# The decay of the recurrent state as a task of its own in a hand-written scheduler, with new ranks and look-ahead

## The chip, the cores and the metric

The kernel runs on one core of a Trainium2 chip. The metric is the device time of one execution in microseconds (us); smaller is better. Where several runs are given, the median counts.

## The reference

Two stages. First a linear recurrence for 4 batches, 8 heads, 768 steps and head size 48: a complex decay per step and per row of the state, normalised so that its magnitude stays below 0.999, and an outer product of key and value added at each step; the output is the query applied to the real part of the state. Then a feed-forward layer on the 3072 tokens of width 384, with 2048 hidden channels and a leaky ReLU.

```python
mag = np.sqrt(a_re * a_re + a_im * a_im)
scale = np.minimum(mag, 0.999) / (mag + 1e-06)
a_re_n, a_im_n = (a_re * scale, a_im * scale)
for t in range(S):
    ar, ai = (a_re_n[:, :, t, :, None], a_im_n[:, :, t, :, None])
    new_re = ar * S_re - ai * S_im
    new_im = ar * S_im + ai * S_re
    kv = np.einsum('bhd,bhe->bhde', k[:, :, t], v[:, :, t])
    S_re, S_im = (new_re + kv, new_im)
    y[:, :, t] = np.einsum('bhd,bhde->bhe', q[:, :, t], S_re)
...
h = x @ w_in
g = np.maximum(0.01 * h, h)
return g @ w_out
```

The weights come as 64-bit floats, and the kernel itself turns them into two 32-bit parts each, a high and a low one.

## The kernel before

The sequence is cut into 6 chunks of 128 steps. A chunk is done for two batches at a time, so there are 12 units of work, numbered n = 0 to 11; n = 0 and 1 are chunk 0 of the two pairs of batches, n = 2 and 3 chunk 1, and so on. Unit n and unit n - 2 share a state. For each unit:

- `prep(n)` turns the decays into running products and scales queries and keys with them. It is a long chain, mostly on VectorE (DVE) with steps on ScalarE (ACT). Its first half writes to the tiles sq, u, a and xs; its second half begins with the first write to the tile qkt, of which there is one, so that it waits until the relays of unit n - 1 have read it.
- `relay_of(n, 0)` and `relay_of(n, 1)` move queries and keys by DMA from qkt to the tile t (t96), with the channels of a head on the partitions.
- `attend(n)`: scores on TensorE (PE, tile att), a mask on DVE (asb, more), keys turned by PE and copied by ACT (kn, more), the output of the unit by PE (att from asb, v and from t, rst), split into a high and a low part x by ACT and DVE, and the new state: PE makes the sum of key times value, DVE adds it to the state rst (`summed_up`), and ACT multiplies the state by the decay of the chunk (`decayed`). `decayed` issues 8 ACT instructions for one batch, one per head, in one go. In chunk 0 there is no old state, and `decayed` reads the sum straight from PSUM.

Beside these, 21 weight units are converted (`convert(i)`, tiles stage_...: ACT, DVE, ACT, PE, ACT), in memory that later holds other tiles; a task that needs such memory waits for the conversions in it (`freed`). The feed-forward layer (`forward`, 12 groups of 256 tokens, one per unit) is one task on PE: `first(g, s)` makes a 512-wide block of hidden values in PSUM (ph), `hide` (ACT, DVE, ACT, DVE, tiles tg and hid) applies the leaky ReLU and splits the result, `second(g, s)` multiplies by the second weight matrix (po). There are two PSUM buffers for ph. `hide(0, s)` for s = 0 to 2 waits for the conversions whose stage memory the tile hid takes over. After the last preparations a check of the weights (wck) runs on DMA and ACT.

The order of the instructions on each engine is written by a planner at build time. Every part above is a `Task` that hands out its instructions step by step (`yield`), and `drive` picks the next step by a clock of estimated costs: it takes the earliest possible start t0, and then, among the steps for the same engine that could start before t0 plus a tolerance, the one of lowest rank:

```python
t0, first = min(free, key=lambda x: (x[0], x[1].rank))
near = [(t.rank, at, k) for k, (at, t) in enumerate(free) if t.lane == first.lane and at <= t0 + look(t.rank)]
t = free[min(near)[2]][1]
```

So a low rank goes first; `look(rank)` is how long an engine may stand idle for it. After each step the rank grows by the task's pace. `DUE` gives rank and pace of the preparations, `UNIT` rank of the first conversion and the distance between two conversions. On a step of one task behind its own earlier step on the same engine the planner puts a start 0.14 to 0.15 us after that engine is free. A step marked "+" is ready as soon as the engine is. On the chip each engine then runs its instructions in this order.

Of the kernel before, what the change touches and what calls it, by code (L numbers as in the profile page):

```python
# [13 lines left out]
AF = mybir.ActivationFunctionType  # L14
# [3 lines left out]
B, H, S, D = 4, 8, 768, 48  # L18
# [3 lines left out]
P = 128  # L22
C = 128
# [15 lines left out]
SUBS = [(0, (0, 1))]  # L39
# [17 lines left out]
QKT, T96, X0, X1, V, A, KN, STG, ST, HID = (0, 1), (2, 3), 4, 5, 6, 7, 8, 9, 10, (11, 12, 13)  # L57
# [12 lines left out]

TOKENS = [(c, b) for c, bs in SUBS for b in bs]

R_RELAY, R_ATT, R_HID, R_FF, R_WCK, R_FLAG = -4, -3, -2, 1000, 10000, 10001
DUE = [(-2, 0.0), (28, 0.7), (250, 0)]
UNIT = (-1.1, 0.5)
PLACE = (8, 10, 11)
LATE = 1
LOOK = {R_RELAY: 0.2, R_ATT: 0.3, -1: 0.16}
SOON = 0.06


def look(rank):
    return SOON if 0 < rank < 200 else LOOK.get(rank, 0.0)

TB = 2

# [70 lines left out]
def pe_costs():  # L157
    small = [False]

    def cost(name, kw, aps):  # L160
        out, n = aps[0], aps[0].free_size()
        tiled = out.partition_size() == 32
        turn = 0.13 if tiled != small[0] else 0.0
        small[0] = tiled
        if name == "transpose":
            each = 0.083
        elif tiled:
            each = 0.029 if n <= D else 0.008 + n * 0.00037
        else:
            each = n * 4 / 2400 if kw["lhsT"].dtype == F32 else n / 2400 + 0.0075  # L170
        return turn + each, turn + each + 0.17

    return cost
# [282 lines left out]
def body(ctx, tc, keep, a_in, qk_in, v_in, w_in, out):  # L456
# [25 lines left out]
    pe, dve, act = Lane(tc, nc.tensor, pe_costs()), Lane(tc, nc.vector, dve_cost), Lane(tc, nc.scalar, act_cost)  # L482
# [26 lines left out]
    banks = Banks(att)  # L509
# [43 lines left out]
    live = []  # L553
    fetched_a, fetched_qk, fetched_v, prepared, moved_q, moved_k, attended, hidden, stored, checked = ({} for _ in range(10))
    converted = []
    carried, scaled, spread, inverted, asked, opened, loading = ([Mark() for _ in SUBS] for _ in range(7))
    placed = {(n, k): Mark() for n in range(2, nsub) for k in range(len(PLACE))}
    cleared = [Mark() for _ in range(NT // GT)]
    summed = [Mark() for _ in range(NT // GT)]

    def task(gen, rank, pace=0.0, end=0.0):
        live.append(Task(gen, rank, pace, end))
        return live[-1]

    def due(n):
        return DUE[n] if n < len(DUE) else (DUE[-1][0] + n, 0)

    def attends_of(n):
        return [attended[n]]

    def fetch_a(n):
        yield "S", *([prepared[n - 2], moved_k[n - 2]] if n > 1 else freed(A) if n else []), *([loading[n - 1]] if n else [])
# [38 lines left out]
    def freed(*places):  # L611
        return [x for x, r in zip(converted, ROUND) if r in places]
# [296 lines left out]
    def slot_of(s, h):  # L909
        if h < 6:  # L910
            return 6 * (h % 2) + 3 * s + h // 2
        return 12 + 2 * s + h - 6
# [16 lines left out]
    def attend(n):  # L929
        c, bs = SUBS[n]  # L930
        nb = len(bs)
        u0 = SUB_POS[n] // C
        g = u0 // NGU
        carry = c < NCH - 1
        at = [[placed[n, k]] if n > 1 else [] for k in range(3)]
        once, late = n > 0, n < LATE
        halves = [(bi, hh) for bi in range(nb) for hh in range(2)]
        ps, am, kn, px, pu = {}, {}, {}, {}, {}
# [71 lines left out]
        def update(bi):  # L1010
            v = raw_v[n]
            flat = pu[bi].rearrange("p a b -> p (a b)")
            for h in range(H):
                o = VW + h * D
                for q in range(3):
                    mm(
                        flat[32 * q : 32 * q + 32, h * D : (h + 1) * D],
                        lhsT=kn[bi][:, h].rearrange("p l d -> p (l d)")[:, 32 * q : 32 * q + 32],
                        rhs=v[:, bi, o : o + D],
                        start=True,  # L1020
                        stop=True,
                    )
# [8 lines left out]
        def rest(bi):  # L1031
            xh, xl, x0 = xgroup(u0 + bi)
            dve.scalar_tensor_tensor(
                out=xl[:, :, x0 : x0 + C], in0=px[bi][:, 0:TI], scalar=XSC, in1=xh[:, :, x0 : x0 + C].bitcast(F32),
                op0=ALU.mult, op1=ALU.subtract,
            )
            split[u0 + bi].set(attended[n].end + 0.6)
            banks.give(px.pop(bi), attended[n].end + 0.6)

        def state(bi):  # L1040
            r0 = rst[:, bs[bi], 0, 0]
            return bass.AP(r0.tensor, r0.offset, [list(r0.ap[0]), [PAIR, H // 2], [64, 2], [1, D]])

        def fresh(bi):
            return pu[bi].rearrange("p a b -> p (a b)")[0:96, 0:DM].rearrange("p (k j e) -> p k j e", j=2, e=D)

        def summed_up(bi):
            dve.tensor_tensor(out=state(bi), in0=fresh(bi), in1=state(bi), op=ALU.add)
            banks.give(pu.pop(bi), attended[n].end + 0.6)

        def decayed(bi):
            t96 = relay[n][1]
            r = state(bi)
            src = fresh(bi) if c == 0 else r
            for h0 in (0, 1, 6):
                hn = 2 if h0 == 6 else 3
                s0 = slot_of(1, h0)
                for x in range(hn):
                    h = h0 + (x if h0 == 6 else 2 * x)
                    act.activation(  # L1060
                        r[:, h // 2, h % 2], src[:, h // 2, h % 2], AF.Copy, scale=t96[:, s0 + x, bi, C : C + 1]
                    )
            if c == 0:
                banks.give(pu.pop(bi), attended[n].end + 2.5)

        yield "P", moved_q[n], moved_k[n], *at[0], *(attends_of(n - 1) if n else [masked]), banks.some(4 if once else 1)
        scored = []
        for k, (bi, hh) in enumerate(halves):
            if k:
# [9 lines left out]
        if carry and not late:  # L1079
# [9 lines left out]
            yield "+N"  # L1089
            shown_to = after(act, 0.15)  # L1090
        yield "+P", shown_to, fetched_v[n], banks.some(2 if late or not carry else 4), *at[2], *(
            [summed[g - 2]] if g > 1 else freed((X0, X1)[g])
        )
        for bi in range(nb):
            px[bi] = banks.take()
# [17 lines left out]
        for bi in range(nb):  # L1113
            yield "+V", rounds[bi]
            rest(bi)
        if not carry:
            return
        if late:
            for bi in range(nb):
# [8 lines left out]
            for bi in range(nb):  # L1128
                yield "+P" if bi else "P", banks
                pu[bi] = banks.take()  # L1130
                update(bi)
        for bi in range(nb if c else 0):
            yield "+V"
            summed_up(bi)
        for bi in range(nb):
            yield "+A" if bi else "A"
            decayed(bi)

    NS = NFC // NF
    shown = {}  # L1140
# [111 lines left out]
    masked = task(masks(), R_HID, end=4.5)  # L1252
    for n in range(nsub):
        fetched_a[n] = task(fetch_a(n), UNIT[0] + 5.5 * UNIT[1] if n == 1 else R_RELAY + 0.5)
        fetched_qk[n] = task(fetch_qk(n), R_HID if n else UNIT[0] + 2.5 * UNIT[1])
        prepared[n] = task(prep(n), *due(n))
        if n == 0:
            for i in range(NU):
                converted.append(task(convert(i), UNIT[0] + i * UNIT[1]))
        fetched_v[n] = task(fetch_v(n), R_RELAY - 1 if n else UNIT[0] + 9.5 * UNIT[1])  # L1260
        moved_q[n] = task(relay_of(n, 0), R_RELAY)
        moved_k[n] = task(relay_of(n, 1), R_RELAY)
        attended[n] = task(attend(n), R_ATT)
# [90 lines left out]
```

## Time and profile before

| what | us |
|---|---|
| median of 3 runs | 603.14 |
| lowest, highest run | 597.68, 604.97 |
| the profiled execution, its own time | 599.82 |
| span of the profiled execution | 598.1 |
| PE busy, DVE busy, ACT busy in it | 551.6, 522.6, 388.4 |

The span is the time from the first to the last instruction of the profiled execution. A busy PE is one with a matmul in its pipeline; the columns of a view are said where its rows stand.

### The profile page before, as it was taken

The numbers are of one execution on the slowest core, as the hardware profiler recorded it, in microseconds if no ns is written. First come the engines' busy times: TensorE is split into PE (matmuls) and PEld (weight loads), VectorE is DVE, ScalarE is ACT, GpSimd is POOL, SyncE is SP. The second block draws the span as 40 slices with busy tenths as digits, with TensorE's granted clock in tenths as the row PEclk, the third lists the DMA queues.
The fourth block names the chain that finished last, engine by engine and source line by source line (L and its number), as shares of the span: only waits on it lengthen the run. The fifth ranks groups of instructions, "written<-read, shape, count | busy, mean of one in ns | idle before, by whom it ended". The sixth has DMA issues, their size and how long they took to land.

```text
span 598.1 us, 17875 instructions
## 1 busy us (share of the span) xinstructions
PE 551.6 (92%) x7650; PEld 522.3 (87%) x7650; DVE 522.6 (87%) x897; ACT 388.4 (65%) x862; POOL 5.0 (1%) x23
## 2 busy tenths in 40 slices
PE   3865699999979899999999999999999999998996
PEld 2433499989969899999999999999999998998996
DVE  5999989999989999889999999999999998764232
ACT  7988586475474584584583674764755756775975
POOL 2000000000000000000000000000000000000000
PEclk9895799999999999999999999999999999999999
DMA  8973612522522423234235125125134266356650
GB/s 347 391 234 95 203 59 55 161 85 55 169 76 63 153 83 109 108 106 133 99 101 159 61 80 161 61 82 160 59 95 147 66 175 182 124 157 214 216 180 29
DMA packets 28370, 79.18 MB, mean 132 GB/s; under 512 B 3200, under 2 KB 9344, under 8 KB 28288
## 3 DMA queue, kind: packets, MB, share of 16 engines
q1 hardware_dynamic: 28288, 78.02, 41.1%
q8 instruction: 60, 0.98, 0.7%
q14 instruction: 22, 0.18, 0.1%
HBM read 54.26 MB, written 4.72 MB: 99 GB/s over the span
## 4 chain that ended last, share of the span: by engine, by line
PE 58%; DVE 20%; ACT 11%; DMA 7%; issue 3%; SPq 0%; DVEq 0%; ACTq 0%
PE po L121 21%; PE ph L121 20%; PE att L121 15%; DVE qkt L121 5%; DVE a L121 4%; DMA wck<-in_w_dram 3%; ACT wck L121 3%; DVE tg L121 2%; DMA t<-qkt 2%; DVE u L121 2%; DVE hid L121 2%; ACT rst L121 2%; DVE sq L121 1%; PE pd L121 1%; ACT tg L121 1%
## 5 line engine op out<-in xcount | busy, mean ns | idle before, releaser
L121 PE MATMUL ph<-x,win_hi 128*128 128x256 f32 x1152 | 215.7, 279 | 5.3 <-DVE tg L121 2.0
L121 PE MATMUL po<-hid,wout_hi 128*128 128x256 f32 x1152 | 215.3, 280 | 0.0
L121 PEld LDWEIGHTS ph<-x,win_hi 128*128 128x128 f32 x1152 | 181.4, 188 | 6.9 <-DVE tg L121 2.4
L121 PEld LDWEIGHTS po<-hid,wout_hi 128*128 128x128 f32 x1152 | 180.7, 188 | 1.6 <-issue 0.4
L121 PE MATMUL ph<-x,win_lo 128*128 128x256 f32 x576 | 141.6, 278 | 0.0
L121 PE MATMUL po<-hid,wout_lo 128*128 128x256 f32 x576 | 137.3, 278 | 0.0
L121 PEld LDWEIGHTS po<-hid,wout_lo 128*128 128x128 f32 x576 | 108.5, 188 | 0.0
L121 PEld LDWEIGHTS ph<-x,win_lo 128*128 128x128 f32 x576 | 108.4, 188 | 0.0
L121 ACT CAST hid<-tg 128x512 fp32r<-128x512 f32 x96 | 59.2, 616 | 52.7 <-DVE tg L121 50.9
L121 DVE TENSOR_TENSOR tg<-ph,tg 128x512 f32<-128x512 f32 x96 | 66.0, 687 | 30.5 <-ACT tg L121 30.4
L121 ACT ACTIVATE tg<-ph 128x512 f32<-128x512 f32 x96 | 56.7, 591 | 39.2 <-PE ph L121 38.9
L121 DVE TENSOR_TENSOR hid<-tg,hid 128x512 fp32r<-128x512 f32 x96 | 66.1, 688 | 14.2 <-ACT hid L121 13.3
L121 DVE TENSOR_TENSOR u<-a 128x384 f32<-128x384 f32 x84 | 46.6, 555 | 1.7 <-ACT a L121 0.2
L121 DVE TENSOR_TENSOR qkt<-qk,a 128x768 f32<-128x768 f32 x48 | 44.4, 956 | 2.6 <-ACT qkt L121 2.6
L121 PE MATMUL att<-t 96*32 96x96 f32 (+3 forms) x1536 | 36.9, 254 | 4.1 <-DMA t<-qkt 3.9
L121 PEld LDWEIGHTS att<-t 96*32 96x32 f32 x1536 | 33.8, 145 | 7.7 <-DMA t<-qkt 4.6
L121 PE MATMUL att<-t,rst 96*32 96x128 f32 x640 | 34.4, 272 | 1.6 <-issue 1.6
L121 ACT ACTIVATE wck<-wck 128x1152 f32<-128x1152 f32 (+1 forms) x22 | 27.2, 1238 | 11.5 <-DMA wck<-in_w_dram 11.4
L121 PE MATMUL att<-asb,v 128*32 128x128 f32 x592 | 33.9, 274 | 0.3 <-issue 0.3
L121 ACT ACTIVATE rst<-rst,t 96x48 f32<-96x48 f32 x128 | 29.8, 321 | 4.6 <-DVE rst L121 4.4
L121 DVE TENSOR_TENSOR a<-u 128x192 f32<-128x192 f32 x84 | 29.9, 356 | 1.9
L121 ACT ACTIVATE sq<-a 128x1536 f32<-128x1536 f32 x12 | 17.9, 1495 | 15.4 <-DMA a<-in_a_dram 15.4
(161 smaller groups left out, 769.8 us busy)
## 6 DMA issues: line engine op xcount, KB each, us to landing
t<-qkt SPq DMA_DIRECT2D x48, 290.2 KB, 4.2
wck<-in_w_dram SPq DMA_DIRECT2D x10, 1152.0 KB, 5.7
v<-in_v_dram SPq DMA_DIRECT2D x12, 832.0 KB, 4.7
a<-in_a_dram SPq DMA_DIRECT2D x12, 768.0 KB, 4.6
qk<-in_qk_dram SPq DMA_DIRECT2D x12, 768.0 KB, 5.9
out_dram<-ot SPq DMA_DIRECT2D x12, 384.0 KB, 2.7
t<-qkt SPq DMA_DIRECT2D x24, 129.0 KB, 4.1
stage_st<-in_w_dram SPq DMA_DIRECT2D x3, 768.0 KB, 4.5
```

The lines of the kernel that those rows point to most:

```text
L121: x = getattr(self.engine, name)(*args, **kw)
```

## The change

The decay leaves `attend` and becomes a task `fade` that issues one ACT instruction per step, 16 in a unit, with rank `R_FADE` = -3.142. `attend(n)` ends before it. The mark `faded[n]` stands for its end: the load of v and the relay of the queries of the next unit wait for it as they waited before for the end of `attend`, and the output matmuls of unit n wait for `faded[n - 2]` where they depended through the order of the units before; the scores of the next unit no longer wait for the decay. In chunk 0 (n = 0 and 1) the sum is first copied from PSUM to the state by ACT, one copy per batch, and the decay then reads the state in SBUF: 4 copies are added in all, and 32 of the 160 decays read another memory.

The ranks are set anew. `prep(0)` keeps -2 but now sinks by 0.078 a step, `prep(1)` goes from 28 (pace 0.7) to -9.02 (pace 0.201), the later ones from 250, 253, 254 ... to 244.623, 280.36, 284.36 ...; the conversions go from -1.1 + 0.5 i to 1.423 + 0.702 i. The tolerances change too: 0.2 to 0.417 for relays, 0.3 to 0.087 for attention, 0 to 0.199 for the steps of `hide` and `store`, 0 to 0.122 for all other negative ranks, 0.06 to 0.105 for ranks between 0 and 200.

```diff
-R_RELAY, R_ATT, R_HID, R_FF, R_WCK, R_FLAG = -4, -3, -2, 1000, 10000, 10001
-DUE = [(-2, 0.0), (28, 0.7), (250, 0)]
-UNIT = (-1.1, 0.5)
+R_RELAY, R_ATT, R_HID, R_FADE, R_FF, R_WCK, R_FLAG = -4, -3, -2, -3.142, 1000, 10000, 10001
+DUE = [(-2, -0.078), (-9.02, 0.201), (244.623, 0), (280.36, 0)]
+UNIT = (1.423, 0.702)
...
-LOOK = {R_RELAY: 0.2, R_ATT: 0.3, -1: 0.16}
-SOON = 0.06
+LOOK = {R_RELAY: 0.417, R_ATT: 0.087, R_HID: 0.199}
+EARLY, SOON, LATER = 0.122, 0.105, 0
 def look(rank):
-    return SOON if 0 < rank < 200 else LOOK.get(rank, 0.0)
+    if rank in LOOK:
+        return LOOK[rank]
+    return EARLY if rank < 0 else SOON if 0 < rank < 200 else LATER if rank < 900 else 0.0
...
     def attends_of(n):
-        return [attended[n]]
+        return [attended[n], faded[n]]
...
-        def decayed(bi):
+        def fade():
             t96 = relay[n][1]
...
+            for bi in range(nb):
+                r = state(bi)
+                for h in range(H):
+                    yield "+A" if bi or h else "A"
                     act.activation(
-                        r[:, h // 2, h % 2], src[:, h // 2, h % 2], AF.Copy, scale=t96[:, s0 + x, bi, C : C + 1]
+                        r[:, h // 2, h % 2], r[:, h // 2, h % 2], AF.Copy, scale=t96[:, slot_of(1, h), bi, C : C + 1]
                     )
-            if c == 0:
-                banks.give(pu.pop(bi), attended[n].end + 2.5)
+            yield "+N"
+            faded[n].set(act.clock + 0.3)
...
-        yield "P", moved_q[n], moved_k[n], *at[0], *(attends_of(n - 1) if n else [masked]), banks.some(4 if once else 1)
+        yield "P", moved_q[n], moved_k[n], *at[0], *([attended[n - 1]] if n else [masked]), banks.some(4 if once else 1)
...
-        for bi in range(nb if c else 0):
-            yield "+V"
-            summed_up(bi)
         for bi in range(nb):
-            yield "+A" if bi else "A"
-            decayed(bi)
+            yield "+V" if c else "A"
+            if c:
+                summed_up(bi)
+            else:
+                act.copy(state(bi), fresh(bi))
+                banks.give(pu.pop(bi), attended[n].end + 0.6)
+        yield "+N"
+        task(fade(), R_FADE, end=attended[n].end)
```

## Rows read from the trace of the kernel before

**Rows 1.** The page: busy time by engine; the span in 40 slices, busy tenths.
```profile
PE 551.6 (92%) x7650; PEld 522.3 (87%) x7650; DVE 522.6 (87%) x897; ACT 388.4 (65%) x862; POOL 5.0 (1%) x23
...
PE   3865699999979899999999999999999999998996
...
DVE  5999989999989999889999999999999998764232
...
```

**Rows 2.** Windows of the whole core: stretch, length, busy time of each engine.
```profile
0.00:77.40 77.40, 48.20 (x328) 27.95 (x329) 70.01 (x117) 61.18 (x115) 3.80 (x13) 0.85 0.70 246
77.40:165.00 87.60, 84.86 (x1222) 82.84 (x1223) 84.06 (x150) 52.21 (x129) 0.24 (x2) 1.00 0.34 102
165.00:250.00 85.00, 78.37 (x1231) 76.17 (x1225) 79.76 (x134) 50.28 (x123) 0.24 (x2) 1.00 0.34 102
250.00:500.00 250.00, 249.04 (x3834) 246.27 (x3822) 238.97 (x404) 156.30 (x375) 0.72 (x6) 1.00 0.37 110
```

**Rows 3.** Window of DVE alone before the feed-forward starts: stretch, length, busy time.
```profile
7.00:77.40 70.40, 68.08 (x110) 0.83 0.69 243
```

**Rows 4.** Timeline of DVE, 33 to 69 us: start, length, operation, [idle before it].
```profile
33.26 0.56 DVE L121 SCALAR_TENSOR_TENSOR stage_hid<-stage_hid 128x384 int32<-128x384 int32 x1
...
53.62 2.43 DVE L121 SCALAR_TENSOR_TENSOR stage_hid<-stage_hid 128x384 int32<-128x384 int32 x5
...
68.60 0.56 DVE L121 SCALAR_TENSOR_TENSOR stage_stg<-stage_stg 128x384 int32<-128x384 int32 x1
```

**Rows 5.** Timeline of SP and PE: relay of keys, first scores, first feed-forward matmul.
```profile
62.37 4.00 SPq L121 DMA_DIRECT2D t<-qkt  x5
...
68.50 3.67 PE L121 MATMUL att<-t 96*32 96x128 f32 x128
...
77.44 0.28 PE L121 MATMUL ph<-x,win_hi 128*128 128x256 f32 x1
```

**Rows 6.** Timeline of DVE, 77 to 106 us: operations of prep(1).
```profile
77.55 0.56 DVE L121 TENSOR_TENSOR u<-a 128x384 f32<-128x384 f32 x1
...
83.80 0.33 DVE L121 TENSOR_TENSOR xs<-u 128x48 f32<-128x48 f32 x2
...
86.17 1.75 DVE L121 TENSOR_TENSOR qkt<-a 128x1536 f32<-128x1536 f32 x1
...
103.98 1.83 DVE L121 TENSOR_TENSOR qkt<-qk,a 128x768 f32<-128x768 f32 x2
```

**Rows 7.** Timeline of ACT: two blocks of decays, and what follows the second.
```profile
122.40 3.10 ACT L121 ACTIVATE rst<-att,t 96x48 f32<-96x48 f32 x16
...
171.95 3.73 ACT L121 ACTIVATE rst<-rst,t 96x48 f32<-96x48 f32 x16 [2.42 <-DVE rst L121]
175.58 0.57 ACT L121 ACTIVATE tg<-ph 128x512 f32<-128x512 f32 x1
```

**Rows 8.** Timeline of DVE: the wait just behind the first of these blocks.
```profile
125.99 1.76 DVE L121 TENSOR_TENSOR qkt<-a 128x1536 f32<-128x1536 f32 x1 [0.55 <-ACT a L121]
```

**Rows 9.** The chain that ended last: its stretches of decays; start, length, what.
```profile
122.50 3.01 ACT rst L121 x16
...
173.32 2.35 ACT rst L121 x10
...
216.70 1.58 ACT rst L121 x7
...
467.45 3.48 ACT rst L121 x15
```

**Rows 10.** Groups of ACT: a copy of 384 columns; count, busy, mean ns.
```profile
L121 ACT COPY kn<-att 128x384 f32<-128x384 f32 x20 | 8.8, 481 | 7.4 <-PE att L121 7.3
```

**Rows 11.** Timeline of PE, 115 to 182 us: three of the gaps.
```profile
117.58 0.31 PE L121 MATMUL att<-ident,t 96*128 96x96 f32 x1 [0.88 <-issue]
...
124.45 0.74 PE L121 MATMUL ph<-x,win_hi 128*128 128x256 f32 x4 [0.93 <-DVE x L121]
...
176.93 0.39 PE L121 MATMUL ph<-x,win_hi 128*128 128x256 f32 x1 [1.74 <-DVE tg L121]
```

More of the change, by code (lines that the diff above doesn't have):

```diff
@@ L555, in body @@
     converted = []
-    carried, scaled, spread, inverted, asked, opened, loading = ([Mark() for _ in SUBS] for _ in range(7))
+    faded, carried, scaled, spread, inverted, asked, opened, loading = ([Mark() for _ in SUBS] for _ in range(8))
     placed = {(n, k): Mark() for n in range(2, nsub) for k in range(len(PLACE))}
@@ L1049, in summed_up @@
             banks.give(pu.pop(bi), attended[n].end + 0.6)
-        def decayed(bi):
+        def fade():
             t96 = relay[n][1]
[L1053 to L1059, printed above, removed]
+            for bi in range(nb):
+                r = state(bi)
+                for h in range(H):
+                    yield "+A" if bi or h else "A"
                     act.activation(
-                        r[:, h // 2, h % 2], src[:, h // 2, h % 2], AF.Copy, scale=t96[:, s0 + x, bi, C : C + 1]
+                        r[:, h // 2, h % 2], r[:, h // 2, h % 2], AF.Copy, scale=t96[:, slot_of(1, h), bi, C : C + 1]
                     )
-            if c == 0:
-                banks.give(pu.pop(bi), attended[n].end + 2.5)
-        yield "P", moved_q[n], moved_k[n], *at[0], *(attends_of(n - 1) if n else [masked]), banks.some(4 if once else 1)
+            yield "+N"
+            faded[n].set(act.clock + 0.3)
+        yield "P", moved_q[n], moved_k[n], *at[0], *([attended[n - 1]] if n else [masked]), banks.some(4 if once else 1)
         scored = []
@@ L1091, in attend @@
         yield "+P", shown_to, fetched_v[n], banks.some(2 if late or not carry else 4), *at[2], *(
-            [summed[g - 2]] if g > 1 else freed((X0, X1)[g])
+            [summed[g - 2], faded[n - 2]] if g > 1 else freed((X0, X1)[g])
         )
@@ L1116, in attend @@
         if not carry:
+            faded[n].set(attended[n].end)
             return
```

## The prediction

> **What bounds the kernel now.** I read the page first, then the windows, then the timelines around the start of the feed-forward layer, and the chain last. On the page PE is busy 551.6 and DVE 522.6 of 598.1 us, and the digits of the slices change places: DVE stands at 9 from the second slice on to about 500 us, PE only from the sixth or seventh, and at the end PE stays at 9 while DVE falls [rows 1]. The windows give this in numbers [rows 2]. Until 77.4 us the feed-forward layer has not begun and PE is idle for 77.4 - 48.2 = 29.2 us. From 77.4 to 250 us PE is idle for 2.7 + 6.6 = 9.4 us, from 250 to 500 us for 1.0 us. So from 250 us on PE is the bound, and whatever it has not done by then comes at the end. Before 250 us it is DVE that holds PE back: from 7 to 77.4 us it is idle for 70.4 - 68.1 = 2.3 us [rows 3], and from there to 250 us for 3.5 + 5.2 = 8.8 us [rows 2]. The change takes no DVE instruction away. What a new order can win is therefore bounded: DVE can finish the work that PE waits for at most 2.3 + 8.8 = 11.1 us sooner, if all its idle time in this stretch went and PE could use it. ACT is busy 65% [rows 1] and counts only where its queue delays one of the other two.
>
> **The decay as a task.** The same 160 multiplications remain. Rank -3.142 lies below attention (-3), `hide` (-2) and all later preparations (244 and more), and a low rank goes first. A step of `fade` is marked "+", so it is ready the moment ACT is free, when nothing else on ACT can start earlier. Every time one of the 16 steps is to be chosen, it wins; only `prep(1)` in its first 30 steps and the later part of `prep(0)` rank lower, and these are over by then. So I expect the 16 decays of a unit to stand together in ACT's queue as before: a block of 3.10 us in chunk 0 and 3.73 us behind [rows 7], begun at the same event, the state's sum from DVE. What waits behind it is the same: the activation that empties ph comes at 175.58 us right after a block, and PE gets its next buffer at 176.93 us after a wait of 1.74 us [rows 7, 11]. Value taken: 0. The bound on the gain is the block's whole place in the chain, 3.01 + 2.35 + 1.58 + 3.48 = 10.4 us [rows 9]; the bound on the loss is nothing, for no decay is added. The scores of the next unit lose a wait that was over long before in the order of the queue: 0.
>
> **Chunk 0.** Four copies of 96 x 384 from PSUM are added. A copy of 384 columns takes 481 ns [rows 10], two of them about 0.85 us as they overlap. The 16 decays behind now read SBUF, as those of the later chunks: 3.73 instead of 3.10 us [rows 7]. Together 0.85 + 0.63 = 1.5 us of ACT for each of units 0 and 1. After the block of unit 1 DVE waits 0.55 us for an ACT copy that stood behind it [rows 8], so 1.5 us more lands on DVE there. For unit 0 the same can happen to the first `hide`. Bounds 0 and 3.0 us; I take 1.0, since PE has gaps of its own in this stretch [rows 11] that swallow a part.
>
> **prep(1) before the conversions.** This is the real reordering. Before, `prep(1)` with rank 28 filled what prep(0), attention and the conversions left. After 33.26 us DVE still has 24 conversion operations, 14.6 us, the last at 68.60 us [rows 4]; they alternate with prep(0), whose next step is never ready at once, and one run of five takes 2.43 us where prep(0) waits for ACT [rows 4]. The feed-forward layer starts at 77.44 us, after the scores of unit 0 (68.50 us) [rows 5]. So the conversions have 77.4 - 69.2 = 8.3 us in hand. Now `prep(1)` takes these places. How much is it? At 77.55 us its first half has only the operations up to 83.80 us to go, about 5.6 us without the one `tg` and the gap in them; its second half, 12 operations from 86.17 to the two that start at 103.98 us, sums to 13.3 us [rows 6]. The second half cannot start before the relay of unit 0 has read qkt, 62.37 + 4.00 us and a landing later [rows 5]. So at most 5.6 + 13.3 = 18.9 us of DVE work can come in front of conversions that PE and `hide` need, and 8.3 us of this are in hand. The other 10.6 us are the bound on a later start of group 0. But that work is only moved: after group 0 DVE has as much less to do for unit 1, whose attention then fits inside group 0, and PE's 9.4 us of gaps until 250 us shrink by what it lost before. The net lies between +10.6 - 9.4 = +1.2 us and the gain of the gaps of unit 1, 0.88 + 0.93 us [rows 11] and a little more, if the start does not move. I take -2.0 us: each step of `prep(1)` needs 0.14 us after its last, so conversions still get every other place, and I expect the start within 4 us of 77.4.
>
> **The tolerances.** On a chain within one engine a next step is ready after 0.14 us, and 0.122 and 0.105 us are below that, so there they change nothing. They act where a step comes from another engine: DVE may idle up to 0.199 us for a `hide` step rather than begin a preparation of about 1 us. PE does 163.2 of the 503.4 us that it works after 77.4 us before 250 us [rows 1, 2], a third, so some 32 of the 96 hidden blocks lie there; two DVE steps for each, 0.2 us each, are 12.8 us if all waited. An estimate: a step arrives inside a window of 0.2 us before an operation of 1 us one time in five, and half the window is waited, so 64 x 0.2 x 0.1 = 1.3 us. Against that, PE's blocks come sooner by the operation not put before them, and attention waits less (0.087 for 0.3 us). Bounds +3 and -5 us; I take -1.0. The new ranks from prep(2) on keep their order among themselves: 0.
>
> **The sum.** 599.82 + 0 + 1.0 - 2.0 - 1.0 = 597.8 us against the profiled execution. The median of the runs is 3.3 us higher and the lowest run 2.1 us lower; a median of the new kernel may fall anywhere in that spread. I forecast 598 us. No change that a measurement can tell reaches from 591 to 615 us, 2% to either side of the median of 603.14.
>
> **Rivals.** (1) The hand-out does what it says: the activations of `hide` slip between the decays, the four places in the chain go [rows 9], and DVE's waits behind them too. The page "Perfetto Trace Analysis" of the Trainium skill, section Optimizing Scalar/DVE Operations, says that where Scalar and Vector are not saturated but cause bubbles on other engines, breaking up instructions may let work finish sooner; the decays are separate instructions already, so by that rule the gain is that of the order. With all DVE idle time as its ceiling the time is 599.8 - 10.4 = 589.4 us, with the tolerances 585 to 591. For it: the 1.74 us gap of PE behind a block [rows 7, 11]. Against: the rank. Chance 0.2. (2) The slow one: the conversions of the stage memory used two and three times, which `hide(0, s)` and the keys of unit 0 wait for, slip behind all 18.9 us of `prep(1)`. Group 0 stops for want of hid, unit 0's attention ends late, and the relay for unit 1 waits for it. It decides from the point where PE's gaps until 250 us, 9.4 us [rows 2], no longer take the delay up. With the 10.6 us of above wholly lost the time is 599.8 + 10.6 = 610 us; if prep(0) too is held, because `prep(1)` ranks below it for its first 20 steps, the 8.3 us in hand do not count and all 18.9 us are lost, 619 us. For it: DVE has no idle time there [rows 3]. Against: the alternation. Chance 0.12. (3) Nothing measurable moves, since DVE is as full as before and everything is only exchanged: 600 to 604 us; this is so near the forecast that they share one chance, 0.68.
>
> **How the numbers follow.** The forecast with rival 3 reaches from 592 to 607 us. To leave no more than 2 in 10 out, the range goes into rival 1 down to 587 and into rival 2 up to 611. Below 591 us lie most of rival 1 and a little of the forecast: 0.18. Above 615 us lies the upper end of rival 2: 0.05. The rest, 0.77, is within 2%.
>
> **What would show it.** Decays in the new trace: 16 in one block, about 3.7 us also in chunk 0, with 4 copies of 384 columns to rst before the first two; if `tg` or `hid` stand between them, rival 1 is right. First matmul of ph between 75 and 82 us; beyond 88 us, rival 2. The second half of prep(1) done by about 90 us instead of 105.8. DVE idle before 250 us still 8 to 13 us, and PE idle from 250 to 500 us about 1 us. I am wrong if PE's gaps after 250 us grow, for then the later ranks, which I put at nothing, have moved something, or if the total of PE's busy time itself changes.

## The result, and the profile after

The changed kernel takes 609.14 us (median of 4 runs, 606.59 to 610.73) against 601.78 us of the kernel before beside it (4 runs, 597.68 to 604.97): ratio 1.0123, 95% interval 1.0081 to 1.0165. It is slower by a little over 1%, inside the forecast range and within the 2%, where I had forecast 598 us, a gain. The profiled execution after took 609.05 us, its span is 607.3 us; before 599.82 and 598.1 us.

The page of the changed kernel (busy time by engine; busy tenths in 40 slices; the group of the decays), beside [rows 1]:

```profile
PE 552.4 (91%) x7650; PEld 522.2 (86%) x7650; DVE 521.4 (86%) x897; ACT 390.6 (64%) x866; POOL 5.0 (1%) x23
...
PE   4763599989999989999999999999999999998995
...
DVE  5999899979969999999999999999898998864232
...
L123 ACT ACTIVATE rst<-rst,t 96x48 f32<-96x48 f32 x160 | 37.2, 321 | 1.1 <-DVE rst L123 1.1
```

PE's busy time has grown by 0.8 us, the span by 9.2; nearly all of it is idle time of PE. Where, the windows say (stretch, length, busy time of PE, PEld, DVE, ACT, POOL; then the granted clock of TensorE as a share of full speed, the share of the DMA engines, GB/s), beside [rows 2]:

```profile
0.00:77.40 77.40, 43.40 (x250) 23.89 (x250) 68.07 (x117) 57.83 (x107) 3.80 (x13) 0.80 0.67 240
77.40:165.00 87.60, 83.37 (x1163) 80.53 (x1162) 79.77 (x134) 54.75 (x133) 0.24 (x2) 0.98 0.33 103
165.00:250.00 85.00, 81.28 (x1263) 78.86 (x1262) 77.80 (x133) 49.77 (x125) 0.24 (x2) 1.00 0.34 101
250.00:500.00 250.00, 247.56 (x3766) 244.89 (x3766) 239.39 (x406) 154.65 (x376) 0.60 (x5) 1.00 0.33 100
```

From 77.4 to 250 us DVE, the engine that holds PE back there, is idle for 7.8 + 7.2 = 15.0 us; before it was 8.8 us. Two waits of DVE make 7.8 us of it. Its timeline shows them (start, length, operation, [idle before it, and what ended it]), with the operation ahead of each wait:

```profile
127.17 1.76 DVE L123 TENSOR_TENSOR qkt<-a 128x1536 f32<-128x1536 f32 x1 [0.54 <-ACT a L123]
132.17 1.76 DVE L123 TENSOR_TENSOR a<-a 128x1536 f32<-128x1536 f32 x1 [3.24 <-ACT a L123]
...
173.32 0.32 DVE L123 TENSOR_TENSOR xs<-u 128x48 f32<-128x48 f32 x2
178.19 1.76 DVE L123 TENSOR_TENSOR qkt<-a 128x1536 f32<-128x1536 f32 x1 [4.56 <-issue]
```

The first stands in prep(2), beside the attention of unit 1, the second in prep(3), beside unit 2. What DVE waits for is read on ACT's timeline at the same times (the last two lines are from the end of the kernel):

```profile
124.79 0.85 ACT L123 COPY rst<-att 96x384 f32<-96x384 f32 x2
126.72 0.36 ACT L123 COPY a<-xs 128x96 f32<-128x96 f32 x1 [1.09 <-DVE xs L123]
126.90 3.71 ACT L123 ACTIVATE rst<-rst,t 96x48 f32<-96x48 f32 x16
130.52 0.90 ACT L123 ACTIVATE ot<-po 128x256 f32<-128x256 f32 x3
131.31 0.58 ACT L123 ACTIVATE tg<-ph 128x512 f32<-128x512 f32 x1
131.79 0.35 ACT L123 COPY a<-xs 128x96 f32<-128x96 f32 x1
...
172.96 3.72 ACT L123 ACTIVATE rst<-rst,t 96x48 f32<-96x48 f32 x16 [1.08 <-DVE rst L123]
176.59 0.90 ACT L123 ACTIVATE ot<-po 128x256 f32<-128x256 f32 x3
177.39 0.54 ACT L123 COPY a<-xs 128x96 f32<-128x96 f32 x2
...
600.26 0.94 ACT L123 ACTIVATE ot<-po 128x256 f32<-128x256 f32 x3 [1.50 <-PE po L123]
601.07 1.31 ACT L123 ACTIVATE wck<-wck,low 128x1152 f32<-128x1152 f32 x1
```

`prep` ends its first half with two copies a<-xs of 96 columns; DVE goes on only behind them. In unit 1 the block of 16 decays has come between the two, with ot and tg behind it; in unit 2 the block and ot stand ahead of both. The second wait is put down to "issue", but the copies end at 177.39 + 0.54 = 177.93 us, 0.26 us before DVE goes on. That it waits for them is inferred from ACT's timeline; in the kernel before the view names them for the same operation, with a wait of 0.54 us (last line below). The kernel before had the same block [rows 7], but in unit 2 not in that place; its ACT timeline, and one line of DVE's:

```profile
165.45 0.54 ACT L121 COPY a<-xs 128x96 f32<-128x96 f32 x2 [1.61 <-DVE xs L121]
...
591.29 1.36 ACT L121 ACTIVATE wck<-wck,low 128x1152 f32<-128x1152 f32 x1
...
592.97 0.94 ACT L121 ACTIVATE ot<-po 128x256 f32<-128x256 f32 x3 [0.24 <-PE po L121]
...
165.90 1.76 DVE L121 TENSOR_TENSOR qkt<-a 128x1536 f32<-128x1536 f32 x1 [0.54 <-ACT a L121]
```

There the copies of prep(3) begin 6.5 us before the block does, at 171.95 us [rows 7]. With the new ranks the last xs comes at 173.6 us and not at 165.4, while the block begins only 1 us later than before: the preparation has moved behind the attention, and the block is ready first.

The starts of the scores of each unit on PE (us) show what these places cost; the last columns are two experiments of below:

| unit | before | after | fourth | thirteenth |
|---|---|---|---|---|
| 0 | 68.5 | 74.0 | 74.5 | 74.3 |
| 1 | 111.0 | 112.7 | 114.0 | 113.1 |
| 2 | 154.7 | 158.6 | 156.7 | 152.2 |
| 3 | 196.4 | 204.0 | 196.5 | 194.6 |
| 5 | 281.4 | 289.1 | 282.4 | 281.6 |

After is 1.7 us late at unit 1, 3.9 at unit 2, 7.6 at unit 3 and 7.7 at unit 5. The rest arises at the end: from the start of the last ot to the end of the span it is 598.1 - 592.97 = 5.1 us before and 607.3 - 600.26 = 7.0 us after. 7.7 + 1.9 is about the 9.2 us. PE shows both: its gap behind the first wait of DVE, where [rows 11] had 1.74 us at the most, and its last wait, before the flag of the check:

```profile
134.59 0.39 PE L123 MATMUL ph<-x,win_hi 128*128 128x256 f32 x1 [2.65 <-DVE tg L123]
...
603.82 0.19 PE L123 MATMUL att<-scr 128*1 128x1 f32 x2 [3.48 <-DVE scr L123]
```

In the kernel before that last wait is 1.02 us. The windows show one thing more that the prediction had no term for, the granted clock of TensorE; the first line is the kernel before, the others the changed one:

```profile
77.40:593.00 515.60, 503.19 (x7322) 494.24 (x7320) 451.42 (x768) 326.13 (x744) 1.20 (x10) 1.00 0.38 116
```
```profile
135.20:138.60 3.40, 3.40 (x19) 3.40 (x18) 3.40 (x6) 3.18 (x5) 0.00 (x0) 0.50 0.00 0
138.60:142.00 3.40, 3.40 (x31) 3.40 (x31) 2.84 (x5) 2.80 (x5) 0.00 (x0) 1.00 0.07 19
...
558.50:561.90 3.40, 3.40 (x50) 2.95 (x43) 1.54 (x3) 2.98 (x8) 0.00 (x0) 0.50 0.14 16
```

Before the change the clock is full, 2.4 GHz, from 77.4 us to the last po. In the changed kernel it is at half, 1.2 GHz, in two stretches: one begins just behind the gap of 2.65 us, the other just behind a gap of 2.00 us that ends at 557.26 us. In the first PE comes to 19 matmuls of ph and po, in the next 3.40 us at full clock to 31; by this the first stretch costs some 1.3 us, an estimate.

### The profile page after: what moved, and what is told of

Read it like the earlier page. It is cut to its first block, busy times and chain, and to the rows that moved or that the text cites. A ratio compares the mean times of both kernels' runs of the same rounds, so it can differ in the third digit from the quotient of the medians.

```text
span 607.3 us, 17861 instructions
## 1 busy us (share of the span) xinstructions
PE 552.4 (91%) x7650; PEld 522.2 (86%) x7650; DVE 521.4 (86%) x897; ACT 390.6 (64%) x866; POOL 5.0 (1%) x23
## 4 chain that ended last, share of the span: by engine, by line
PE 44%; DVE 9%; ACT 5%; DMA 2%; issue 2%; SPq 1%; DVEq 0%; ACTq 0%
PE po L123 18%; PE ph L123 17%; PE att L123 9%; DVE qkt L123 2%; DMA wck<-in_w_dram 2%; ACT wck L123 2%; DVE tg L123 1%; ACT rst L123 1%; DVE a L123 1%; SPq L123 1%; DVE hid L123 1%; DVE u L123 1%; ACT hid L123 1%; DVE sq L123 1%; DVE xs L123 1%
## 5 line engine op out<-in xcount | busy, mean ns | idle before, releaser
L123 ACT ACTIVATE rst<-rst,t 96x48 f32<-96x48 f32 x160 | 37.2, 321 | 1.1 <-DVE rst L123 1.1
L123 PE MATMUL att<-t 96*32 96x32 f32 (+3 forms) x1536 | 34.9, 250 | 1.0 <-DMA t<-qkt 0.9
L123 PEld LDWEIGHTS att<-t 96*32 96x32 f32 x1536 | 32.4, 144 | 3.7 <-DMA t<-qkt 1.6
L123 ACT ACTIVATE x<-att 128x384 fp32r<-128x384 f32 x24 | 11.8, 492 | 26.8 <-PE att L123 26.8
```

What stands on the lines that cost most here:

```text
L123: x = getattr(self.engine, name)(*args, **kw)
```

## The experiments

Three theories were set against each other. A: the block of decays stands on ACT ahead of small operations that DVE waits for. B: `prep(1)` pushes the conversions back, the feed-forward layer starts later (81.28 us, before 77.44 [rows 5]), and that start is lost. C: the task itself, its copies and marks, costs. "Before" is the kernel before on the same chip.

**1. The ranks alone.** The kernel before with the new ranks and tolerances; the decay stays in `attend`.

```diff
-DUE = [(-2, 0.0), (28, 0.7), (250, 0)]
-UNIT = (-1.1, 0.5)
+DUE = [(-2, -0.078), (-9.02, 0.201), (244.623, 0), (280.36, 0)]
+UNIT = (1.423, 0.702)
...
-LOOK = {R_RELAY: 0.2, R_ATT: 0.3, -1: 0.16}
+LOOK = {R_RELAY: 0.417, R_ATT: 0.087, R_HID: 0.199}
```

> The kernel before with the new ranks and tolerances alone; the decay stays in attend. Theory A (the loss is the block of decays standing on ACT in front of two small copies a<-xs that DVE waits for, at units 1 and 2): here the block stands before one pair of copies only (unit 1), one DVE wait of about 3 us instead of two of 3.2 and 4.6 us, so 604 to 606 us. Theory B (prep(1) pushes the conversions back and the feed-forward starts later, 81.3 instead of 77.4 us): all of the loss, 608 to 610 us. Theory C (the task itself, its rank above attention and its four copies): none of it, 601 to 603 us.

Measured 625.22 us (622.42 to 629.55), ratio 1.0346, 1.0263 to 1.0429: worse than any of the theories said. From unit 3 to unit 9, seven times, ACT and DVE show the same picture:

```profile
348.45 3.72 ACT L123 ACTIVATE rst<-rst,t 96x48 f32<-96x48 f32 x16 [2.81 <-DVE rst L123]
352.07 0.58 ACT L123 ACTIVATE tg<-ph 128x512 f32<-128x512 f32 x1
352.55 0.53 ACT L123 COPY a<-xs 128x96 f32<-128x96 f32 x2
```
```profile
352.68 0.69 DVE L123 TENSOR_TENSOR tg<-ph,tg 128x512 f32<-128x512 f32 x1 [3.17 <-ACT tg L123]
```

Here tg and both copies stand behind the block in each unit, and DVE waits 3.2 to 3.6 us each time; in the kernel before it has no wait over 1.1 us from 77 to 300 us. It is theory A in a larger dose, and it needs no task. From the first ph to the last po PE is also busy for 512.2 us with the matmuls that take it 504.9 us in the changed kernel, at a mean granted clock of 0.98 for 0.99.

**2. The task alone.** The changed kernel with the old ranks and tolerances, 0.3 for the decay.

```diff
-DUE = [(-2, -0.078), (-9.02, 0.201), (244.623, 0), (280.36, 0)]
-UNIT = (1.423, 0.702)
+DUE = [(-2, 0.0), (28, 0.7), (250, 0)]
+UNIT = (-1.1, 0.5)
...
+LOOK = {R_RELAY: 0.2, R_ATT: 0.3, -1: 0.16, R_FADE: 0.3}
```

> The changed kernel with the ranks and tolerances of before; the decay is a task of rank -3.142. Theory A: the block stands before the copies a<-xs at units 1 and 3 and behind them at unit 2; one or two DVE waits of 2 to 4 us, 603 to 606 us. Theory B: no loss, 601 to 603 us, first ph matmul at about 77 us. Theory C: all of it, 608 to 610 us.

Measured 622.1 us (621.39 to 624.12), ratio 1.0291, 1.023 to 1.0352. From 218 to 493 us DVE waits 3.7 us for tg seven times, once in each unit, and ACT's timeline has a block ahead of each tg. Either half of the change alone puts the block ahead of both copies a<-xs, and of the tg that DVE then waits for, in every unit from 3 to 9; in the changed kernel tg stands behind the block there too, but the copies stand ahead of it, so that DVE has work, and its only wait over 1 us in that stretch is one of 1.36 us.

**3. prep(1) late again.** The changed kernel with the old ranks of prep(1) and of the conversions. The expectation names a pace of 0.201 for prep(1); the edit has the old 0.7.

```diff
-DUE = [(-2, -0.078), (-9.02, 0.201), (244.623, 0), (280.36, 0)]
-UNIT = (1.423, 0.702)
+DUE = [(-2, -0.078), (28, 0.7), (244.623, 0), (280.36, 0)]
+UNIT = (-1.1, 0.5)
```

> The changed kernel with rank 28 (pace 0.201) for prep(1) and the old ranks of the conversions. Theory A: at unit 1 the block stands between the two copies, at unit 2 behind them; one DVE wait of about 3 us, 604 to 606 us. Theory B: the loss is gone, 600 to 603 us, first ph matmul at 76 to 78 us. Theory C: 608 to 610 us.

Measured 614.0 us (613.09 to 615.07), ratio 1.0161, 1.01 to 1.0223. The feed-forward layer starts at 74.18 us, 7.1 us earlier, and the kernel is not faster: B falls. The copies of prep(2) are again split by the block (a wait of 2.44 us), and PE has a gap of 3.81 us at 136.60 us for tg. That it is 5 us slower than the changed kernel is more than A had said. The windows from the first ph to the last po add it up; the first line is the changed kernel, the others this run:

```profile
81.30:600.30 519.00, 504.92 (x7325) 495.23 (x7323) 448.21 (x755) 328.36 (x748) 1.20 (x10) 0.99 0.37 115
```
```profile
74.20:605.20 531.00, 510.80 (x7332) 502.08 (x7330) 455.08 (x772) 329.32 (x749) 1.20 (x10) 0.99 0.36 113
116.90:127.10 10.20, 8.93 (x183) 8.36 (x178) 9.19 (x22) 4.02 (x10) 0.00 (x0) 0.50 0.47 162
```

PE is idle for 20.2 us and not 14.1, and busy 5.9 us longer with nearly the same matmuls; less the 7.1 us of earlier start this is 4.9 us. Behind a gap of 2.76 us, in which PE waits for the relays of unit 1 until 114.64 us, the granted clock is at half for 10.2 us, and again behind the gap of 3.81 us. So the early start is lost to waits, one of them not theory A's, and to the slow clock behind them.

**4. The decays last.** The changed kernel with one number changed: at 500 whatever else is ready on ACT goes before a decay, except the check of the weights.

```diff
-R_RELAY, R_ATT, R_HID, R_FADE, R_FF, R_WCK, R_FLAG = -4, -3, -2, -3.142, 1000, 10000, 10001
+R_RELAY, R_ATT, R_HID, R_FADE, R_FF, R_WCK, R_FLAG = -4, -3, -2, 500, 1000, 10000, 10001
```

> The changed kernel with rank 500 instead of -3.142 for the decay, so that every other step on ACT goes first. Theory A: the DVE waits of 3.2 and 4.6 us behind the decays go, 600 to 603 us, although the feed-forward still starts at about 81 us. Theory B: 608 to 610 us. Theory C: the copies stay, the rank goes, 605 to 608 us.

Measured 599.79 us (596.86 to 601.4), ratio 0.9942, 0.9908 to 0.9975: 9.3 us less than the changed kernel, whose interval lies well above, with a start at 81.82 us. ACT at unit 2:

```profile
168.64 0.53 ACT L123 COPY a<-xs 128x96 f32<-128x96 f32 x2 [3.74 <-DVE xs L123]
...
172.08 0.91 ACT L123 ACTIVATE ot<-po 128x256 f32<-128x256 f32 x3
...
173.70 0.79 ACT L123 ACTIVATE rst<-rst,t 96x48 f32<-96x48 f32 x3
174.37 0.59 ACT L123 ACTIVATE tg<-ph 128x512 f32<-128x512 f32 x1
174.85 1.70 ACT L123 ACTIVATE rst<-rst,t 96x48 f32<-96x48 f32 x7
176.44 0.62 ACT L123 CAST hid<-tg 128x512 fp32r<-128x512 f32 x1
```

The copies go ahead of the decays, ot too, and tg and hid slip between. The table above shows where the gain lies: this kernel is 3.0 us behind the kernel before at unit 1, 2.0 at unit 2 and 0.1 at unit 3.

**5. The two blocks left out.** The order of the changed kernel, without the instructions of the decays of units 1 and 2.

```diff
+                    if n in (1, 2):
+                        act.log.append((0.145, 0.245))
+                        continue
```

> Changed kernel with the 16 decays of unit 1 and the 16 of unit 2 left out (the state of these two units is not multiplied by its decay); the planner still counts their time, so the order of all other instructions is the changed kernel's. Theory A (the two blocks that stand on ACT ahead of the small copies a<-xs cost 3.2 and 4.6 us of DVE waits, and all of the loss): both waits gone, 609 - 7 = 601 to 603 us, and the scores of unit 3 begin near 197 us, not 204. Theory C (the blocks cost nothing; the loss is in the rest of the order): 608 to 610 us, scores of unit 3 still at 203 to 204 us.

Measured 603.77 us (600.22 to 611.32), ratio 1.0002, 0.9965 to 1.0039. The time lies just above A's range. But the scores of unit 3 begin at 202.8 us, near where C put them, and both waits have only become shorter; ACT, then DVE:

```profile
174.51 0.94 ACT L123 ACTIVATE ot<-po 128x256 f32<-128x256 f32 x3 [3.75 <-PE po L123]
175.31 0.55 ACT L123 COPY a<-xs 128x96 f32<-128x96 f32 x2
```
```profile
132.69 1.76 DVE L123 TENSOR_TENSOR a<-a 128x1536 f32<-128x1536 f32 x1 [2.29 <-ACT a L123]
...
176.14 1.76 DVE L123 TENSOR_TENSOR qkt<-a 128x1536 f32<-128x1536 f32 x1 [3.04 <-issue]
```

So A has to be said more exactly. The 3.7 us of the block are 0.95 and 1.52 us of the waits; the rest is the place of the copies. The planner, which holds ACT taken until the end of the block, sets ot ahead of the copies as well, and ot waits 3.75 us for PE.

The trace adds to this. The scores of unit 0 begin at 75.29 us here, 1.3 us later than in the changed kernel; from there to unit 3 it is 127.5 us and not 130.0, 2.5 us less, as much as the two waits have lost. Another 2.7 us are won behind unit 3, where nothing was left out: PE has no gap there like the changed kernel's of 1.28 us at 465.43 us, and the granted clock stays full to the last po. So by the medians the two blocks are worth 5.4 us, by the waits 2.5; the way from the blocks to the later 2.7 us is not shown.

**6. The other blocks left out.** The same for units 3 to 9.

```diff
+                    if 2 < n < 10:
+                        act.log.append((0.145, 0.245))
+                        continue
```

> Changed kernel with the 16 decays of each of units 3 to 9 left out (112 of the 160; the state of these units is not multiplied by its decay), the order of all other instructions kept. Theory A: in these units the copies a<-xs stand ahead of the block and DVE waits for none of them, so nothing is won: 607 to 610 us. Rival (any block costs by its length, wherever it stands): 7 blocks of 3.7 us against 2, so 609 - 7 x 3.7 = 583 us if all of it counts, and below 600 us if half does.

Measured 607.95 us (606.02 to 612.25), ratio 1.0106, 1.007 to 1.0141. Without 112 of the 160 decays the time stays, to 1.2 us: seven blocks that stand behind the copies cost next to nothing. (One wait of DVE, for tg at 471.50 us, is longer here, 3.56 us for 1.36, and may hide a small gain.) DVE's two waits are as they were:

```profile
133.48 1.76 DVE L123 TENSOR_TENSOR a<-a 128x1536 f32<-128x1536 f32 x1 [3.24 <-ACT a L123]
...
178.72 1.76 DVE L123 TENSOR_TENSOR qkt<-a 128x1536 f32<-128x1536 f32 x1 [4.55 <-issue]
```

**7. Old ranks, decays last.** The second experiment with R_FADE = 500.

> Kernel of the second experiment (decay as a task, ranks and tolerances as before the change), with the rank of the decay task at 500 and not -3.142. Theory A: the 20 us that the second experiment lost come from the block that stands ahead of the copies a<-xs and of tg in every unit from the fourth on; with the block gone 598 to 604 us, and DVE's waits for tg fall from 28.8 us below 6. Theory C (the task itself, its four copies, or its other marks cost them): it stays above 612 us.

Measured 607.78 us (602.3 to 612.32), ratio 1.0084, 1.0036 to 1.0132. 14 of the 20 us that the second experiment lost are back by this one number, so the task and its copies didn't cost them; C falls. The last 4 us to A's range are not. In the profiled execution, which took 604.34 us, DVE waits 6.6 us for tg in eleven pieces between 77 and 510 us, and PE 4.4 us for the relays between 77 and 250 us (2.5 us of it ahead of unit 2). That execution is not one that shows the lost 4 us: in the ten runs the time goes with the mean granted clock, 602.3 to 604.3 us at 0.979 to 0.983, 607.0 to 612.3 us at 0.970 to 0.977.

**8. Decays last, prep(1) late.** The fourth experiment with prep(1) at (28, 0.7) and the conversions at (-1.1, 0.5).

> Kernel of the fourth experiment (rank of the decay task 500) with the ranks of prep(1) and of the conversions as before the change: the feed-forward layer should start near 77 us or earlier, not at 81.8. Theory A: the start does not matter, since the gaps behind it take it up, 598 to 602 us. Theory B (each us of later start is lost at the end): 4 to 7 us less than the fourth experiment's 599.8, 593 to 596 us.

Measured 600.74 us (599.0 to 604.18), ratio 0.9998, 0.9959 to 1.0038. The first ph comes at 75.33 us, 6.5 us before that of the fourth experiment, and the end is no earlier: B falls a second time.

**9. Decays last in units 1 and 2 alone.**

```diff
-        task(fade(), R_FADE, end=attended[n].end)
+        task(fade(), 500 if n in (1, 2) else R_FADE, end=attended[n].end)
```

> Changed kernel with the rank of the decay task at 500 in units 1 and 2 alone; in the other units it stays at -3.142, and the 16 decays of each stay one block. Theory A (the loss lies in the order of ACT's queue in these two units, where the block and the ot behind it stand ahead of the copies a<-xs): as the fourth experiment, 599 to 603 us, with the scores of unit 3 near 197 us and not 204. Rival (the fourth experiment won in every unit a little, by smaller pieces): 605 us or more.

Measured 606.66 us (4 runs, 602.48 to 610.63), ratio 1.0101, 1.0049 to 1.0153: A's time is missed. The scores of unit 3 do begin at 194.6 us, but the next block, that of unit 3, now stands ahead of hid, and DVE waits 3.13 us there; ACT, then DVE:

```profile
211.21 3.71 ACT L123 ACTIVATE rst<-rst,t 96x48 f32<-96x48 f32 x16
214.83 0.60 ACT L123 CAST hid<-tg 128x512 fp32r<-128x512 f32 x1
```
```profile
215.46 0.69 DVE L123 TENSOR_TENSOR hid<-tg,hid 128x512 fp32r<-128x512 f32 x1 [3.13 <-ACT hid L123]
```

**10. The planner told the true cost of a decay**, 0.232 us (3.71 / 16) for its 0.145.

```diff
+    if kw.get("scale") is not None and hasattr(kw["scale"], "free_size"):
+        long += 0.087
```

> Changed kernel, ranks as they are; the planner's cost of an ACT activation with a scale per partition is raised by 0.087 us to what the trace shows for a decay (3.71 us for 16). In the order that follows, the two copies a<-xs of unit 2 stand ahead of the block, those of unit 1 are still split by it, now with two tg in between. Theory A: the wait of 4.6 us goes, the one of 3.2 us stays or grows, 604 to 606 us. Rival (the place of the copies does not matter): 608 to 610 us.

Measured 608.36 us (604.12 to 612.26), ratio 1.0096, 1.0055 to 1.0138, above A's 604 to 606 us and no different from the changed kernel. The wait in prep(3) is gone; the one in unit 1 is now 5.60 us, for tg behind the block. A planner with better costs, but with the same rank, finds another victim.

**11. The old tolerances.** The changed kernel with 0.2, 0.3 (attention and decay), 0 and 0.06.

> Changed kernel with the tolerances of the kernel before (0.3 for the decay too). The order that follows has the copies a<-xs of unit 2 ahead of the block, and in unit 1 both of them behind the block and the ot. Theory A: one wait of 4 to 5 us in unit 1 and none in unit 2, 604 to 607 us. Rival (the tolerances themselves win 1 us, as predicted, and losing them costs it; the copies do not matter): 609 to 611 us.

Measured 605.14 us (602.15 to 609.61), ratio 1.0057, 1.0023 to 1.0092. In A's range, and in unit 2 there is no wait, as expected; but besides the wait in unit 1 (3.30 us at 128.13 us, both copies behind the block) there is one in unit 0 (3.24 us at 90.77 us, tg behind the block) and one of 3.93 us at 253.35 us where no block stands. One wait taken away came back elsewhere.

**12. The last store ranked behind the check.** The fourth experiment with rank 20000 for the last store.

> Kernel of the fourth experiment (rank of the decay task 500), with the last store behind the check of the weights: the last copy of wck goes ahead of the last ot on ACT. If that place costs what the chain at the end shows, PE's last wait, 3.48 us, shrinks to 1 to 2 us, and the time is 1.5 to 2 us under the fourth experiment's 599.8: 597 to 599 us. If the last ot and its DMA end last then: 599 to 601 us.

Measured 599.4 us (596.74 to 602.8), ratio 0.996, 0.9933 to 0.9987. The edit left the order of every engine as it was, since ot was ready first on the planner's clock; this is the fourth experiment a second time.

**13. Decays last in units 1 to 4.** As the ninth, with `0 < n < 5`.

> Changed kernel with the rank of the decay task at 500 in units 1 to 4; from unit 5 on it is one block of 16 at -3.142 as in the changed kernel, behind the copies a<-xs in ACT's order. Theory A (a block costs where it stands ahead of what DVE needs next, and nothing elsewhere): as the fourth experiment, 599 to 602 us, scores of unit 5 near 282 us. Rival (a block costs something in each unit): the 6 blocks left cost 605 us or more.

Measured 602.3 us (601.34 to 608.15), ratio 1.0017, 0.9977 to 1.0056. The blocks from unit 5 on stand behind the copies, DVE has one wait over 1 us up to 300 us (1.05 us), unit 5 begins at 281.6 us. Six whole blocks are left, and 6.8 of the 9.3 us are won: a whole block costs little where it stands behind the copies. What the other 2.5 us are is not shown.

**14. Decays last, old tolerances.** The fourth experiment with 0.2, 0.3, 0 and 0.06.

> Kernel of the fourth experiment (rank of the decay task 500) with the tolerances of the kernel before. Theory A (the block is all that mattered; the tolerances are worth the 1 us of the prediction): 600 to 602 us. Rival (once the block is gone, the new tolerances are what brings the fourth and the eighth experiment below the seventh, which had the old ones): 604 to 608 us.

Measured 597.59 us (595.23 to 602.31), ratio 0.9922, 0.9886 to 0.9957. The rival falls, and the new tolerances turn out to cost 2.2 us against the fourth experiment. The two intervals overlap a little, but the trace shows where: PE's last wait is 1.19 us here and 3.48 us in the fourth. The seventh's last 4 us stay open.

**15. The last store behind the check, by a wait.** The fourth experiment with one wait more.

```diff
-        yield "A", *([stored[g - 1]] if g else freed(STG))
+        yield "A", *([stored[g - 1]] if g else freed(STG)), *(checked.values() if g == NT // GT - 1 else [])
```

> Kernel of the fourth experiment with the last store made to wait for the check of the weights, so that the last copy of wck stands ahead of the last ot on ACT, as in the kernel before. If that place costs the 1.9 us by which the end of the changed kernel is longer (7.0 us from the start of the last ot to the end of the span, 5.1 us before the change): 597.5 to 598.5 us, and PE's last wait falls from 3.48 us to 1 to 2 us. If the store then ends last in place of the check: 599 to 600.5 us.

Measured 597.27 us (595.75 to 602.07), ratio 0.9923, 0.9893 to 0.9952. The last copy of wck now goes ahead of ot, and PE's last wait, 3.48 us in the changed kernel and in the fourth experiment, is 1.20 us; ACT, then PE:

```profile
589.54 1.31 ACT L123 ACTIVATE wck<-wck,low 128x1152 f32<-128x1152 f32 x1
...
591.02 0.94 ACT L123 ACTIVATE ot<-po 128x256 f32<-128x256 f32 x3
```
```profile
592.29 0.19 PE L123 MATMUL att<-scr 128*1 128x1 f32 x2 [1.20 <-DVE scr L123]
```

**16. Both.** The fourteenth with the wait of the fifteenth.

> Kernel of the fourteenth experiment (rank of the decay task 500, tolerances of the kernel before) with the last store behind the check of the weights, as in the fifteenth. If the two add: 597.6 - 2 = 595 to 596.5 us. If the order at the end leaves the check behind the store anyway, or the store then ends last: 597 to 598 us.

Measured 597.85 us (594.74 to 600.68), ratio 0.992, 0.9889 to 0.9952. In the fourteenth the check already went first (PE's last wait there: 1.19 us), and this edit moved nothing on any engine: it is that kernel again. Old tolerances and the wait at the end win the same 2 us. At 0.992 both beat the kernel before and, by 11 us, the changed one.

## Why the prediction was wrong

**The decay as a task** is the step that failed. Its first half held: the rank makes the 16 decays one block in each unit, 3.71 us in unit 1 too. The failure is "What waits behind it is the same", and from it "the bound on the loss is nothing, for no decay is added". I weighed how long the block is and when it begins, and not what else becomes ready on ACT just then. The wait of 0.55 us for a copy behind the block of unit 1 had shown it [rows 8]. I used it for 1.5 us more of block and not for the case that the copies of other units change sides. The ranks of the preparations, which I put at nothing, decide that, together with the block. Put right by the fourth experiment, the step is worth 9.3 us; by the thirteenth, 6.8 us of it lie in units 1 to 4. The fourth also lets other operations in between the decays, which the kernel before did not, so that the 9.3 us are more than the way back to the old order. Of the 9.3 us it isn't shown how much is the block's own time: the fifth experiment gives 2.5 us of DVE's 7.8 us of waits to it and the rest to the copies' place, but 5.4 us of the kernel's time. Nor did the prediction have the granted clock, which falls to half behind two gaps of PE. That 609 us lies inside the range is luck: the range reached there for rival 2, which is not what happened.

**Rival 1** named the right lever, and was kept down by the rank for the right reason: nothing slips between the decays at -3.142. With the rank at 500 it does, 599.79 for 609.14 us. The page "Perfetto Trace Analysis" of the Trainium skill, section Optimizing Scalar/DVE Operations, says that where Scalar and Vector aren't saturated but cause bubbles on other engines, breaking up instructions may let work finish sooner. No run here tests it: the decays are single instructions in every version, and what the fourth experiment changes is their order. The rival's 589 us are not reached by any version; the lowest median is 597.27 us. (Its sum calls the chain's 10.4 us all of DVE's idle time, which by the prediction's own rows is 11.1.)

**prep(1) before the conversions.** The start moved by 3.8 us, within the 4 us expected. The second half of prep(1) was not done by 90 us but at 107.0 us (105.8 before [rows 6]): it began at 83.44 us, 2.7 us earlier than before, and then conversions, the last at 95.02 us and not at 68.60 [rows 4], and `hide` came in between. The term of -2.0 us can't be told from nothing: the new ranks of prep(1) and the conversions (fourth against eighth experiment) give 599.79 for 600.74 us, with intervals that overlap. That a late start is taken up by the gaps behind it was right, where no block stands in the way.

**The tolerances**, -1.0 us, had the wrong sign: +2.2 us by the fourteenth experiment. I had looked for them among the hidden blocks; what the traces show of them is the end, where the last ot, ranked as `hide` with a tolerance of 0.199 now, goes ahead of the last copy of wck; that it is this tolerance and not another was not run by itself. The place accounts for the 1.9 us at the end: the fifteenth experiment, which changes it alone, wins 2.5 us by the medians.

**Chunk 0.** The four copies and the block from SBUF are there, 0.85 us for the pair of unit 1, two single copies in unit 0, and 3.71 us a block; their +1.0 us wasn't measured by itself, and in unit 1 it is part of the wait of 3.24 us. **Rival 2** did not come: the slow side was reached by another way, and group 0 did not stop. DVE's idle time, expected at 8 to 13 us before 250 us, is 15.0 us from 77.4 to 250 us alone. PE idle from 250 to 500 us is 2.4 us and not 1.0, the sign that I had named for being wrong about the later ranks; which of them does it was not followed up.

The sum, put right with the terms measured: 597.8 + 7.8 (two waits, if PE loses each in full) + 1.0 (the tolerances' gain taken back) + 1.9 (the end) = 608.5 us, against 609.05. That it comes so near is luck in part: it keeps -2.0 us for prep(1), which no run shows, counts the part of chunk 0 that lies in unit 1's wait twice, and has no term for the clock; by the table PE is 5.9 us later from unit 1 to unit 3, not 7.8. Not settled are why the time of the seventh experiment, 4 us above what the theory gives, varies with the granted clock, and the later 2.7 us of the fifth.

## What to carry to other kernels

In a queue worked through in order, a run of operations that nobody waits for cost next to nothing here behind the small operation that the bottleneck engine needs next, and ahead of it a wait of 3.2 to 4.6 us for a run of 3.7; so before costing such a run at nothing, list what else becomes ready on that engine while it runs, unit by unit. Rank it last and let others in between, rather than first because it is needed by the next unit: in each of four pairs of runs that differ in this rank, two of them in the decay's tolerance too (the fourth, seventh, eighth and fourteenth experiments against the changed kernel and the second, third and eleventh) that was faster. After any change of ranks or tolerances look at the end too, where a check or a store decides with no other work to cover it. And when PE loses more than its gaps, read the granted clock of the stretch behind each gap.

## What the runs showed of the hardware that was not expected

Gaps of PE had slow stretches behind them here. In the changed kernel the granted clock of TensorE was at half, 1.2 GHz, from 135.2 to 138.6 us, behind a gap of 2.65 us, and from 558.5 to 561.9 us, behind one of 2.00 us; in the third experiment from 116.9 to 127.1 us, behind one of 2.76 us. In the kernel before it was full from 77.4 us to the last po. That the gap brings the fall about was not tested by a run of its own.

Sixteen decays of 96 x 48 that read and write SBUF take 3.71 us, 0.232 us each, also where the source had been PSUM with 3.10 us, 0.194 us each [rows 7]: reading the state from SBUF made the same operation slower by a fifth, as the prediction had taken it. Handing them out in pieces of 1 to 8 costs ACT nothing to speak of: it is busy 389.5 us in the fourth experiment and 390.6 us in the changed kernel.
